# Row-tiled attention scores, with the second GEMM split into row halves among them and the attention-times-V work gathered into one stretch per pair of heads

One core of a Trainium2 chip. The metric is the device time of one execution in microseconds (us), median of several runs. The notes on the chip that are quoted as "the Trainium skill" are a set of pages; each is named by its title where it is used.

## The reference

Forgetting attention for 8 batches x 8 heads, 576 tokens, head size 64, feeding a two-layer network with exact GELU on the 4608 resulting rows:

```python
scores = q @ k.T / sqrt(64)
decay  = cum[..., :, None] - cum[..., None, :]      # cum = cumsum(log f)
attn   = softmax(where(causal, -1e9, scores + decay))
x      = (attn @ v)  -> rows of 512 (8 heads x 64)
out    = gelu(x @ w_in) @ w_out                     # 512 -> 2048 -> 512
```

Inputs and output are fp32; the kernel multiplies in bf16 and accumulates in fp32.

## The kernel before

Batches go through TensorE one after another. A batch has two stages: its attention, among whose matmuls the second GEMM of the batch before is strewn as filler so that TensorE hardly waits for the exponentials, and then its first GEMM. Heads are handled in pairs, because two heads of 64 fill the 128 partitions. The scores of a pair use one stationary tile of k for both heads; the q of either head is padded with zeros in the other head's half:

```python
# scores(b, i, t): tile t of pair i
for n, q0, w in STILES[t]:
    for h, qt in enumerate((qA[i], qB[i])):          # zero-padded halves
        nc.tensor.matmul(st[:, h, c:c+w], kT[i][:, K0[n]:K0[n]+P],
                         qt[:, q0:q0+w], start=True, ...)
...
nc.scalar.activation(et[:, :, 0:c], st[:, :, 0:c], Act.Exp, scale=scale)
```

The filler counts say how many second-GEMM matmuls follow each score tile; the attention-times-V work ("AV", 15 matmuls a head) is spread over three places of the next pair:

```python
FILL = [[4, 6, 2, 2], [2, 2, 2, 2], [2, 2, 2, 2], [2, 2, 1, 1], [8, 0, 20]]
# attention(b, fill, counts)
for i in range(HP):
    for t in range(4):
        scores(b, i, t)
        if i and t == 1:   attend(b, i - 1, 0, (0, 1, 2))
        elif i and t == 2: attend(b, i - 1, 0, (3, 4));          normalize(b, i - 1, 0)
        elif i and t == 3: attend(b, i - 1, 1, (0, 1, 2, 3, 4)); normalize(b, i - 1, 1)
        ...
        take(fill, counts[i][t])
```

The pools take eight banks of PSUM, the buffer that matmuls write to: two score tiles of two banks each, two banks for AV, two for the GEMMs. A pool hands a buffer on when its last reader is done.

The softmax here doesn't subtract the row's maximum and nothing guards it: scores larger than these inputs give would overflow.

## Time and profile before

| | before |
|---|---|
| median | 356.84 us (356.57 to 357.11) |
| TensorE busy | 97% of the span |
| a steady batch (first score to first score, batch 3) | 37.42 us |
| of which attention with filler / first GEMM | 23.53 / 13.89 us |
| ScalarE (exponentials, GELU) busy in a steady batch | 25.2 us |

The steady batch is the unit to read: batches 3 to 6 repeat it to 0.01 us, and batch 7 repeats its attention. Its rows, and the lines about mode switches and exponentials, stand in the prediction.

### The profile page before, as it was taken

The page shows a single profiled execution, that of the slowest core. Times are in us where ns is not written, and L with a number is a line of the kernel's source. Part 1 is how long each engine was busy: PE and PEld are TensorE (multiplying, and loading weights), DVE is VectorE, ACT ScalarE, POOL GpSimd, SP SyncE. Part 2 cuts the span into 40 slices and gives each one's busy share as a digit, 9 for nine tenths or more (in the row PEclk, how much of TensorE's full clock was granted, in tenths as well). Part 3 has the DMA queues.
Part 4 walks back from the last instruction along what each step waited for, and adds up shares of the span by engine and source line. Part 5 has one row for each costly group of instructions (what it writes and reads, how often), then busy time and mean ns, then how long its engine had stood idle before and what let it go on. Part 6 is the DMA issues. An engine that isn't in the chain of part 4 may idle for free.

```text
span 356.2 us, 7069 instructions
## 1 busy us (share of the span) xinstructions
PE 346.8 (97%) x2756; PEld 190.7 (54%) x2756; DVE 182.1 (51%) x482; ACT 217.4 (61%) x298; POOL 124.5 (35%) x243
## 2 busy tenths in 40 slices
PE   8998989999999999999999999999999999999995
PEld 3784556544664466445654565446544664444443
DVE  6771984595467625781559145924584361011011
ACT  5697586368854797279826882688457854603600
POOL 7390275406546044804470256215520530000000
PEclk9999999999999999999999999999999999999999
DMA  7999999885997894489639973979310132011013
GB/s 116 169 188 191 190 155 202 183 192 90 205 158 161 146 185 122 95 142 189 144 98 134 188 139 82 174 141 173 76 66 2 45 61 81 2 59 59 2 30 88
DMA packets 103936, 43.85 MB, mean 123 GB/s; under 512 B 82720, under 2 KB 99360, under 8 KB 103904
## 3 DMA queue, kind: packets, MB, share of 16 engines
q1 hardware_dynamic: 86608, 29.26, 40.4%
q0 software_dynamic: 16896, 13.63, 25.6%
q10 hardware_dynamic: 400, 0.52, 0.4%
q8 instruction: 21, 0.34, 0.4%
q14 instruction: 11, 0.09, 0.1%
HBM read 36.85 MB, written 9.44 MB: 130 GB/s over the span
## 4 chain that ended last, share of the span: by engine, by line
PE 94%; ACT 2%; DMA 1%; issue 1%; DVE 1%; POOL 0%; ACTq 0%; DVEq 0%; POOLq 0%
PE ps L404 35%; PE ps L442 35%; PE s L308 13%; PE o L344 8%; ACT e L323 2%; PE ps_f L198 1%; DMA k<-in_k_dram 1%; PE s L317 1%; PE ps_w L187 1%; PE ps_x L380 0%; PE s_t L233 0%; PE ps_t L233 0%; DVE x L360 0%; ACT xt L368 0%; ACT g L416 0%
## 5 line engine op out<-in xcount | busy, mean ns | idle before, releaser
L416 ACT ACTIVATE g<-ps 128x512 bf16<-128x512 f32 x144 | 86.0, 597 | 97.9 <-PE ps L404 97.8
L442 PE MATMUL ps<-w_out_sb,g 128*128 128x512 bf16 (+2 forms) x592 | 143.8, 373 | 0.0
L323 ACT ACTIVATE e<-s 128x896 bf16<-128x896 f32 (+1 forms) x128 | 105.1, 863 | 19.8 <-PE s L308 11.3
L404 PE MATMUL ps<-xT,w_in_sb 128*128 128x512 bf16 x512 | 112.9, 379 | 0.7 <-ACT xT L383 0.6
L325 POOL TENSOR_SCALAR_AFFINE_SELECT e<-e 128x256 bf16<-128x256 bf16 x135 | 53.7, 408 | 118.6 <-ACT e L323 117.7
L404 PEld LDWEIGHTS <-w_in_sb 128*128 128x128 bf16 x576 | 56.0, 97 | 69.2 <-issue 3.9
L451 DVE COPY ot<-ps 128x512 f32<-128x512 f32 (+2 forms) x37 | 25.1, 677 | 105.3 <-PE ps L442 105.0
L442 PEld LDWEIGHTS <-g 128*128 128x128 bf16 x592 | 52.2, 98 | 41.8
L292 POOL TENSOR_TENSOR vw<-v_sb,wT 128x640 bf16<-128x640 f32 x32 | 41.0, 1282 | 45.7 <-PE ps_t L233 15.9
L308 PEld LDWEIGHTS <-kT 128*128 128x128 bf16 x384 | 36.7, 98 | 33.3 <-issue 6.2
L308 PE MATMUL s<-qA,kT 128*128 128x256 bf16 (+2 forms) x192 | 51.9, 282 | 2.1 <-ACT e L323 2.0
L308 PE MATMUL s<-qB,kT 128*128 128x256 bf16 (+2 forms) x192 | 48.6, 282 | 0.0
L344 PE MATMUL o<-vw,e 128*128 128x65 bf16 x960 | 43.5, 194 | 0.5 <-ACT e L323 0.4
L344 PEld LDWEIGHTS <-e 128*128 128x128 bf16 x960 | 39.5, 98 | 7.5 <-ACT e L323 0.5
L359 DVE RECIPROCAL r<-o 128x5 f32<-128x5 f32 x64 | 12.5, 195 | 41.5 <-PE o L344 41.0
L276 DVE COPY kT<-tk 64x288 bf16<-64x288 bf16 x96 | 32.3, 336 | 1.4
L360 DVE TENSOR_TENSOR x<-o,r 128x256 bf16<-128x256 f32 x64 | 27.2, 425 | 2.4 <-DVE r L359 0.2
L276 DVE COPY qB<-tq 64x288 bf16<-64x288 bf16 x48 | 18.8, 391 | 0.6
L370 DVE TENSOR_SCALAR xt<-o,r 64x64 bf16<-64x64 f32 x60 | 17.5, 291 | 1.4
L276 DVE COPY qA<-tq 64x288 bf16<-64x288 bf16 x48 | 17.1, 355 | 1.1
L404 PE MATMUL ps<-tails,w_in_sb 128*128 128x512 bf16 x64 | 14.4, 377 | 0.0
L416 ACT ACT_TABLE_LOAD x8 | 10.3, 1283 | 0.1
(63 smaller groups left out, 124.4 us busy)
## 6 DMA issues: line engine op xcount, KB each, us to landing
out_dram<-ot SPq DMA_DIRECT2D x32, 256.0 KB, 2.2
v_sb<-in_v_dram SPq DMA_DIRECT2D x20, 256.0 KB, 4.7
v_sb<-in_v_dram SPq DMA_DIRECT2D x29, 128.0 KB, 5.4
q<-in_q_dram POOLq DMA_DIRECT2D x6, 576.0 KB, 6.6
k<-in_k_dram POOLq DMA_DIRECT2D x6, 576.0 KB, 9.0
w_in_sb<-in_moe_w_in_dram POOLq DMA_DIRECT2D x4, 512.0 KB, 7.6
w_out_sb<-in_moe_w_out_dram POOLq DMA_DIRECT2D x4, 512.0 KB, 9.6
q<-in_q_dram POOLq DMA_DIRECT2D x4, 144.0 KB, 4.1
```

The source lines that it names most:

```text
L276: nc.vector.tensor_copy(rows[:, odd], src[odd * D : (odd + 1) * D, 2 * i + h].rearrange("d j p -> d p j"),)
L292: nc.gpsimd.tensor_tensor(vw_of[b][:, hs, :, 0:D], v_sb[:, hs, :, :], w.unsqueeze(3).to_broadcast([P, 2, NBLK, D]), Alu.mult,)
L308: nc.tensor.matmul(st[:, h, c : c + w], kT[i][:, K0[n] : K0[n] + P], qt[:, q0 : q0 + w], start=True, stop=not on_pe or c not in SDIAG[t],)
L323: nc.scalar.activation(et[:, :, 0:c], st[:, :, 0:c], Act.Exp, scale=scale)
L325: nc.gpsimd.affine_select(out=et[:, :, c0 : c0 + P], in_=et[:, :, c0 : c0 + P], compare_op=Alu.is_ge, fill=0.0, base=0, pattern=[[0, 2], [ ...
L344: nc.tensor.matmul(o[:, m, :], e_of[b, i, t][:, h, c : c + P], vw_of[b][:, 2 * i + h, n, :], start=(n == 0), stop=(n == m),)
L360: nc.vector.tensor_tensor(x_of[b, i][:, :, h, :], o[:, 0:4, 0:D], r[:, 0:4].unsqueeze(2).to_broadcast([P, NBLK - 1, D]), Alu.mult,)
L370: nc.vector.tensor_scalar(*tail, r[D:P, 4:5], None, Alu.mult)
L404: nc.tensor.matmul(ps, w_in_sb[:, kt, ffb * P : (ffb + 1) * P], src[:, kt, :], start=(kt == 0), stop=(kt == n_dm - 1),)
L416: nc.scalar.activation(g_of[c][ffb], ps, Act.Gelu)
L442: nc.tensor.matmul(pss[ts][:, c0:c1], g_of[c][kt][:, ts * P : (ts + 1) * P], w_out_sb[:, kt, c0:c1], start=(kt == 0), stop=(kt == n_ff - 1),)
L451: nc.vector.tensor_copy(ot[:, c0:c1], pss[ts][:, c0:c1])
```

## The change

The intent: two heads' scores each need only 64 rows of the array. Put on the two row halves, they can run side by side and take half the time, and the padding goes. Since a change between 64-row and 128-row work costs something, the second GEMM's steps among the scores are split as well, into two 64-row halves that accumulate in two banks and are added by VectorE; and the AV work, which needs all 128 rows, is gathered into one stretch per pair, with unsplit steps inside it.

```diff
-            for h, qt in enumerate((qA[i], qB[i])):
+            for h in range(2):
+                d = slice(h * D, (h + 1) * D)
                 nc.tensor.matmul(
                     st[:, h, c : c + w],
-                    kT[i][:, K0[n] : K0[n] + P],
-                    qt[:, q0 : q0 + w],
+                    kT[i][d, K0[n] : K0[n] + P],
+                    qT[i][d, q0 : q0 + w],
 ...
+    STEPS = [16 * "r", "rrrrrrrnnrrrrrnn", "rrrrrrrrrrnnrrrr", 8 * "r" + 8 * "n"]
+    def gemm2_rows(c):
+        for ts, steps in enumerate(STEPS):
+            # two banks: block 0 in the AV pool, 1 and 2 in the GEMM pool, 3 in a score tile
 ...
+            for kt, step in enumerate(steps):
+                last = kt == steps.rindex("r")
+                for r in range(2 if step == "r" else 1):
+                    rows = slice(r * D, (r + 1) * D) if step == "r" else slice(0, P)
+                    nc.tensor.matmul(banks[r], g_of[c][kt][rows, ...], w_out_sb[rows, kt, :], ...)
+                if last:
+                    nc.vector.tensor_copy(ot, banks[1])
+                if kt == n_ff - 1:
+                    nc.vector.tensor_tensor(ot, ot, banks[0], Alu.add)
 ...
+    FILL = [[6, 6, 4, 4], [0, 3, 1, 1], [0, 3, 3, 3], [1, 3, 2, 2], [8]]
+    FILL_AV = [2, 2, 2, 2]
+        def av(i):
+            for h in range(2):
+                attend(b, i, h, (0, 1, 2, 3, 4))
+                normalize(b, i, h)
+                if h == 0:
+                    take(fill, FILL_AV[i])
 ...
+                scores(b, i, t)
+                take(fill, FILL[i][t])
+                if i and t == 1:
+                    av(i - 1)
 ...
+        take(fill, FILL[HP][0])
+        av(HP - 1)
+        take(fill, 6)
+        to_xT(b, HP - 1, nc.vector.tensor_copy, o_psum, "o")
```

Batches 0 and 1 keep their old order (batch 1 as a function of its own, with the unsplit GEMM) and only get the row-tiled scores; the zero fills and half of the q evacuations (copies out of PSUM) go. One more thing moves: from batch 3 on, the kernel before sent the last pair's x through a DMA transpose; now TensorE transposes it (`to_xT`, four matmuls) and VectorE copies the result.

More of the change, by code (lines that the diff above doesn't have):

```diff
@@ L142 @@
     make_identity(nc, ident_fp)
-    qA = [consts.tile([P, S], BF16, name=f"qA{i}") for i in range(HP)]
-    qB = [consts.tile([P, S], BF16, name=f"qB{i}") for i in range(HP)]
+    qT = [consts.tile([P, S], BF16, name=f"qT{i}") for i in range(HP)]
     kT = [consts.tile([P, S], BF16, name=f"kT{i}") for i in range(HP)]
-    def zero_halves(pairs):
-        for i in pairs:
-            nc.vector.memset(qA[i][D:P, :], 0.0)
-            nc.vector.memset(qB[i][0:D, :], 0.0)
     w_in_sb = consts.tile([P, n_dm, d_ff], BF16)
@@ L174 @@
     nc.vector.memset(ones, 1.0)
-    zero_halves(range(2))
     nc.vector.memset(wT[0:D, 4, :], 0.0)
@@ L202, in transposes_first @@
                 )
-        def evac(eng, dst, r0, r1):
-            op = eng.copy if eng is nc.scalar else eng.tensor_copy
-            op(
-                dst[r0:r1, :].rearrange("d (p j) -> d p j", j=JT),
-                ps[r0:r1].rearrange("d j p -> d p j"),
-            )
-        if which:
-            evac(nc.vector, kT[i], 0, P)
-        else:
-            evac(nc.vector if i else nc.scalar, qA[i], 0, D)
-            evac(nc.vector, qB[i], D, P)
+        op = nc.scalar.copy if i == 0 and not which else nc.vector.tensor_copy
+        op(
+            (qT, kT)[which][i].rearrange("d (p j) -> d p j", j=JT),
+            ps.rearrange("d j p -> d p j"),
+        )
     def transposes_pe(b, i, pool):
@@ L239, in transposes_pe @@
             for h in range(2):
-                dst = (qA[i], qB[i])[h] if which == 0 else kT[i]
+                dst = (qT, kT)[which][i]
                 rows = dst[h * D : (h + 1) * D, :].rearrange(
@@ L270, in untangle @@
             for h in range(2):
-                dst = (qA[i], qB[i])[h] if which == 0 else kT[i]
+                dst = (qT, kT)[which][i]
                 rows = dst[h * D : (h + 1) * D, :].rearrange(
@@ L461, in gemm2 @@
             yield
+    STEPS = [16 * "r", "rrrrrrrnnrrrrrnn", "rrrrrrrrrrnnrrrr", 8 * "r" + 8 * "n"]
+    def gemm2_rows(c):
+        for ts, steps in enumerate(STEPS):
+            if ts < n_sub - 1:
+                pool, tag = (m_psum, "m") if ts else (o_psum, "o")
+                banks = [
+                    pool.tile([P, d_model], FP32, tag=tag, name="ps2")
+                    for _ in range(2)
+                ]
+            else:
+                both = s_psum.tile([P, 2, d_model], FP32, tag="s", name="ps2")
+                banks = [both[:, 0], both[:, 1]]
+            ot = o_pool.tile([P, d_model], FP32, tag="ot", name="ot")
+            for kt, step in enumerate(steps):
+                last = kt == steps.rindex("r")
+                for r in range(2 if step == "r" else 1):
+                    rows = slice(r * D, (r + 1) * D) if step == "r" else slice(0, P)
+                    nc.tensor.matmul(
+                        banks[r],
+                        g_of[c][kt][rows, ts * P : (ts + 1) * P],
+                        w_out_sb[rows, kt, :],
+                        start=(kt == 0),
+                        stop=last if r else kt == n_ff - 1,
+                    )
+                if last:
+                    nc.vector.tensor_copy(ot, banks[1])
+                if kt == n_ff - 1:
+                    nc.vector.tensor_tensor(ot, ot, banks[0], Alu.add)
+                    nc.sync.dma_start(
+                        out[c * S + ts * P : c * S + (ts + 1) * P, :], ot
+                    )
+                yield
     def take(gen, n):
@@ L481, in first_attention @@
         transposes(0, o_psum, "o")
-        zero_halves(range(2, HP))
         warm_up(4)
@@ L534, in first_attention, with attention, second_attention @@
         to_xT(0, 3, nc.vector.tensor_copy)
-    FILL = [[4, 6, 2, 2], [2, 2, 2, 2], [2, 2, 2, 2], [2, 2, 1, 1], [8, 0, 20]]
+    FILL = [[6, 6, 4, 4], [0, 3, 1, 1], [0, 3, 3, 3], [1, 3, 2, 2], [8]]
+    FILL_AV = [2, 2, 2, 2]
     FILL_1 = [[0, 4, 4, 0], [0, 2, 3, 3], [4, 4, 4, 4], [3, 3, 3, 3], [8, 0, 99]]
-    def attention(b, fill, counts):
+    def attention(b):
+        fill = gemm2_rows(b - 1)
+        def av(i):
[4 more added lines that the diff above has]
+                    take(fill, FILL_AV[i])
+        for i in range(HP):
+            for t in range(4):
+                scores(b, i, t)
+                take(fill, FILL[i][t])
+                if i and t == 1:
+                    av(i - 1)
+                    if i < HP - 1 or b > 2:
+                        x_dma(b, i - 1)
+                if t == 1 and i == 0:
+                    load_v(b + 1)
+                if b > 2 and t == 0 and i < 2:
+                    transpose_dma(b + 1, 4 * i, 4 * i + 4)
+                if b == 2 and t == 1 and i == 1:
+                    transpose_dma(3, 0, 4)
+                    transpose_dma(3, 4, 8)
+        take(fill, FILL[HP][0])
+        if b == 2:
+            to_xT(b, HP - 2, nc.vector.tensor_copy, o_psum, "o")
+        av(HP - 1)
+        take(fill, 6)
+        to_xT(b, HP - 1, nc.vector.tensor_copy, o_psum, "o")
+        x_tail_dma(b)
+        take(fill, 999)
+    def second_attention():
+        b, fill, counts = 1, gemm2(0, True), FILL_1
         for i in range(HP):
@@ L552, in attention @@
                     normalize(b, i - 1, 1)
-                    if i < HP - 1 or b > 2:
+                    if i < HP - 1:
                         x_dma(b, i - 1)
-                if t == 1 and i == 0 and b > 1:
-                    load_v(b + 1)
-                if b > 2 and t == 0 and i < 2:
-                    transpose_dma(b + 1, 4 * i, 4 * i + 4)
-                if b == 2 and t == 3 and i == 1:
-                    transpose_dma(3, 0, 4)
-                    transpose_dma(3, 4, 8)
-                if b == 1 and (i, t) == (0, 2):
+                if (i, t) == (0, 2):
                     transposes_pe(1, 3, o_psum)
-                if b == 1 and i == 1 and t in (0, 2):
+                if i == 1 and t in (0, 2):
                     weigh_v(1, 2 + t // 2)
-                if b == 1 and t == 3:
+                if t == 3:
                     if i == 1:
@@ L573, in attention @@
         take(fill, counts[HP][0])
-        if b <= 2:
-            to_xT(b, i - 1, nc.vector.tensor_copy, o_psum, "o")
+        to_xT(b, i - 1, nc.vector.tensor_copy, o_psum, "o")
         attend(b, i, 0, (0, 1, 2, 3, 4))
@@ L580, in attention @@
         normalize(b, i, 1)
-        if b <= 2:
-            take(fill, 7)
-            to_xT(b, i, nc.vector.tensor_copy, o_psum, "o")
-        else:
-            x_dma(b, i)
+        take(fill, 7)
+        to_xT(b, i, nc.vector.tensor_copy, o_psum, "o")
         x_tail_dma(b)
-        if b == 1:
-            transpose_dma(2, 4, 8)
-            load_v(2, 4, 8)
+        transpose_dma(2, 4, 8)
+        load_v(2, 4, 8)
         take(fill, 999)
@@ L594 @@
             first_attention()
+        elif b == 1:
+            second_attention()
         else:
-            attention(b, gemm2(b - 1, b == 1), FILL_1 if b == 1 else FILL)
+            attention(b)
         if b == 0:
```

## The prediction

> **What bounds the kernel now.** I read the page first (busy shares, the chain that ended last), then busy time by stage, then one steady stage instruction by instruction.
>
> ```profile
> PE 346.8 (97%) x2756; PEld 190.7 (54%) x2756; DVE 182.1 (51%) x482; ACT 217.4 (61%) x298; POOL 124.5 (35%) x243
> PE 94%; ACT 2%; DMA 1%; issue 1%; DVE 1%; POOL 0%; ACTq 0%; DVEq 0%; POOLq 0%
> ```
>
> The chain is TensorE (PE) almost throughout: first GEMM (line 404) 35%, second GEMM (line 442) 35%, scores (line 308) 13%, attention times V ("AV", line 344) 8%. By stage:
>
> ```profile
> core 0: us, PE busy (x) PEld busy (x) DVE busy (x) ACT busy (x) POOL busy (x), PEclk, DMA share, GB/s
> 0.00:11.10 11.10, 9.41 (x70) 4.95 (x71) 7.32 (x17) 5.57 (x6) 7.08 (x19) 1.00 0.88 134
> 11.10:28.70 17.60, 15.44 (x269) 12.57 (x269) 13.81 (x33) 14.71 (x21) 12.14 (x18) 1.00 1.09 175
> 44.50:71.30 26.80, 25.27 (x263) 15.72 (x261) 16.84 (x45) 16.64 (x19) 16.04 (x30) 1.00 1.03 180
> 146.90:160.80 13.90, 13.90 (x67) 6.29 (x65) 11.86 (x33) 8.96 (x15) 3.09 (x5) 1.00 0.81 144
> 160.80:184.30 23.50, 23.50 (x234) 14.24 (x232) 9.37 (x27) 16.23 (x19) 12.11 (x26) 1.00 0.78 137
> ```
>
> The first two rows are batch 0's attention, the third batch 1's with the second GEMM of batch 0 as filler. The last two are a steady batch, repeated six times (batches 2 to 7): 13.9 us of first GEMM, then 23.5 us of attention filled with the second GEMM. There PE never pauses; everybody else does. Work on PE is what sets a steady stage, though ScalarE's (ACT's) 16.23 us of exponentials and tables is not far below. A busy PE record overlaps its neighbours, so I cost PE by start-to-start distances: 13.89 us for 64 matmuls of 512 columns is 0.217 each (512 columns at 2.4 per ns is 0.213); 15 AV matmuls take 0.48.
>
> Two further details matter. How fast ACT can run, and how long a change of array shape takes:
>
> ```profile
> 162.76 1.73 ACT L323 ACTIVATE e<-s 128x896 bf16<-128x896 f32 x2
> ```
> ```profile
> 11.40 0.28 PE L317 MATMUL s<-after,ident_bf 128*128 128x128 bf16 x2
> 11.61 0.52 PE L489 MATMUL psw<-ident_fp,f_sb 64*128 64x64 f32 x5
> ...
> 12.95 0.27 PE L317 MATMUL s<-after,ident_bf 128*128 128x128 bf16 x2
> 13.15 0.47 PE L198 MATMUL ps_f<-ident_bf,k 96*64 96x96 bf16 x10
> ...
> 14.13 0.28 PE L317 MATMUL s<-after,ident_bf 128*128 128x128 bf16 x2
> 14.24 0.25 PE L308 MATMUL s<-qA,kT 128*128 128x192 bf16 x1
> ```
>
> One wide exponential lasts 0.92, so two in 1.73 start 0.81 apart. Two 128-column mask matmuls should occupy 0.11, as they do ahead of line 308 (14.13 to 14.24). Ahead of the 64-row fp32 matmuls and of the 64-column transposes the distance is 0.21 and 0.20: about **0.10 us more when the shape of the array changes**.
>
> **What the Trainium skill says.** "TensorEngine Tiling (Array Packing)", Key Properties: changing the tiling mode, not merely the tile, drains TensorE. No duration is given; the 0.10 above agrees. The same page, Gotcha 1: different row tiles must write different PSUM banks, which is why the changed GEMM takes two banks per block. "TensorE: Matmul & The Clock Gate", Measured speedup vs the span model: a packed group takes one matmul's time plus about 4 ns per further tile. No concurrent pair exists in the trace before, so I take the 4 ns from there. "PSUM — Partial Sum Buffer", PSUM bank collisions: readers and writers of a bank must be kept apart by semaphores; so a block's banks come free only after VectorE's (DVE's) last read, and that becomes important below.
>
> **The change part by part, one steady stage.**
>
> *Scores.* Each pair of heads has per head 256+192+320+128+448+320 = 1664 columns, now two zero-padded 128-row matmuls in a row. Two heads: 2 x (1664/2.4 + 6 x 2.5 ns) = 1.42 us; as concurrent 64-row tiles 0.73 us. Four pairs: **-2.7 us**.
>
> *Second GEMM.* 50 of its 64 steps become two 64-row halves in two banks: the same 0.217 us each plus 4 ns, +0.2 us. They do no work faster; they keep the array in row mode among the scores.
>
> *Mode switches.* Into row mode at the stage's start, out and back round three AV stretches, out for the fourth: 8 x 0.10 = **+0.8 us**.
>
> *DVE.* Per token block one more 512-column pass (copy one bank, add the other): 4 x 0.69 = +2.8 us on an engine 40% busy. Harmless in sum, not where the next step waits for it.
>
> So by sum a stage falls by 1.7 us, six stages by 10 us. But the order changes too, so I laid the stage out, time 0 at its first score. Rules from the stage before: score finished issuing to exponential 0.29 (169.81 to 170.10); exponential end to the score reusing its buffer 0.05; AV end to DVE 0.19; normalization 0.95; first exponential at 2.11 (last GELU, then table load of 1.28).
>
> - Pair 0, 20 steps, ends at 5.2. The exponentials keep up.
> - Pair 1: scores 0 and 1, three steps, AV from 6.4 to 7.8. Before, the two AV halves lay between different scores. Now score 2 waits behind 3 steps + 30 AV matmuls + 2 steps + two switches, about 2.2 us, while two exponentials cover 1.6. **ACT starves about 1 us**, and the next pair's first two scores then wait 0.7 and 0.4 for their PSUM buffers, with only one filler step between.
> - Pair 2: AV ends at 12.3. The next step is the first of block 2, whose banks are block 1's. DVE runs normalization of head 0 (11.5 to 12.5) before block 1's add (to 13.2). **PE waits 0.7**.
> - Pair 3 to 18.8; the 8 steps of block 3 need a score buffer: 0.2 of waiting, then to 20.8.
> - Last AV with 2 steps, 6 more to 23.6, transposes to 23.8. DVE does the last add (to 24.4) before it copies the transposed x (to 24.9); the first GEMM's fourth matmul needs it and could have run at 24.4: **0.5 lost**.
>
> Stalls: 0.7+0.4+0.7+0.2+0.5 = 2.5. Stage: 23.53 - 2.7 + 0.2 + 0.8 + 2.5 = 24.3 against 23.53, so **+0.75, six times: +4.5 us**.
>
> *Batch 1* keeps the unsplit second GEMM among row-tiled scores: roughly 16 score groups with two switches each, 32 x 0.10 = 3.2 against 2.7 saved: +0.5.
> *Batch 0.* The zero fills (8 x 0.30 on DVE) and three evacuations of 0.76 go. The first score, however, waits for PE's own warm-up (four matmuls of 0.43 from 6.99 to 8.70, the score at 8.67), so the start hardly moves. Row-tiled scores at the slow early pace save 0.4, later ones hide behind exponentials: about -0.5.
> *After batch 7* nothing changes. Sum: 356.8 + 4.5 + 0.5 - 0.5 = 361.3.
>
> **The rivals.**
> (1) *PE's sum wins.* If the tuned placement avoids the stalls, six stages gain 1.7 each: 346 to 348. For it: PE is 23.50 of 23.50 busy and loses 2.7 us of work a stage; whoever chose the steps (five in pair 1, twenty in pair 0) probably tuned them by measurement. Against it: each stall follows from in-order engines and two-buffer pools.
> (2) *ACT becomes the bound.* 2.11 + 13 exponentials' worth (16 exponentials, 4 x (3 x 0.81 + 0.6) = 12.1) + AV, 8 steps and transposes after it (2.9) is 17.2, well under 23. So not its busy time, only its starvation counts.
> (3) *Row tiles don't run side by side fully*, or a switch costs more where a weight load must follow it. Each 0.10 more per switch is 0.8 a stage plus 3 in batch 1, 8 in all: 369. Nothing in the profile before shows a concurrent pair, so this stays open.
>
> **Range and chances.** The layout says 361; rival 1 pulls down by up to 14 and deserves about a fifth, rival 3 pulls up. I put it at 360, with 347 to 369 holding it 8 times in 10. Two per cent is 7.1 us: under 349.7 is faster, over 364.0 slower. Faster 0.19, within 0.55, slower 0.26.
>
> **What would show it.** Right: a steady attention stretch (first score to first GEMM) of 24 to 25 us, with pauses of PE before the first scores of pairs 2, before block 2's first step and in the first GEMM's first group, waiting for ACT, DVE and DVE; score pairs 0 to 10 ns apart; about 0.10 at each change of rows. Wrong: a stretch under 22.5 us with no such pauses (rival 1), row steps well over 0.22 us or switches of 0.2 (rival 3), or batches 0 and 1 moving by more than 2 us.

## The result, and the profile after

The changed kernel took 361.62 us (360.75 to 362.45), against 356.82 for the kernel before in the same rounds: ratio 1.0134, 95% interval 1.0106 to 1.0162. Ratios here and below are the mean time of one kernel's fast runs over that of the other's of the same rounds, so not quite the ratio of the medians. All profiled runs are fast ones; of the others one was slow (x_tail's run of 363.73 us, at a granted clock of 0.981), and it is in that median but not in the ratio.

The page's chain (by engine, then by line), after:

```profile
PE 83%; DVE 7%; ACT 5%; issue 2%; DMA 1%; POOL 0%; ACTq 0%; POOLq 0%
PE ps L392 34%; PE ps L474 21%; PE ps L430 11%; PE s L296 7%; PE o L332 6%; ACT e L311 5%; DVE ot L484 2%; DVE ot L482 2%; PE s L305 1%; PE ps_f L192 1%; DMA k<-in_k_dram 1%; DVE x L348 1%; DVE xT L371 1%; PE ps_w L181 1%; DVE xt L358 0%
```

The scores (now line 296) fell from 13% to 7%, as intended. But 94% TensorE became 83%: VectorE (7%) and ScalarE (5%) now stand in the path that sets the end. The same steady batch, cut at its first score and its first GEMM matmul (columns as in the prediction's table):

```profile
162.41:186.27 23.86, 22.49 (x287) 12.82 (x287) 12.40 (x34) 16.06 (x19) 9.14 (x21) 1.00 0.84 150
186.27:200.58 14.31, 14.07 (x67) 6.17 (x65) 13.81 (x33) 8.96 (x15) 6.19 (x10) 1.00 0.65 107
```

Attention lasts 23.86 instead of 23.53, and TensorE is no longer busy all through it; the first GEMM lasts 14.31 instead of 13.89. Together 38.17 against 37.42: 0.75 more, in each of the batches 3 to 6. Where the time lies idle shows in the order of time. Pairs 1 and 2 of that batch (start, length, instruction, and in brackets the idle time before it and what ended it):

```profile
168.58 0.65 PE L332 MATMUL o<-vw,e 128*128 128x65 bf16 x15
169.07 0.59 PE L474 MATMUL ps<-w_out_sb,g 128*128 128x512 bf16 x2
169.50 0.64 PE L332 MATMUL o<-vw,e 128*128 128x65 bf16 x15
...
170.07 0.36 PE L296 MATMUL s<-qT,kT 64*128 64x448 bf16 x2
...
170.53 3.18 ACT L311 ACTIVATE e<-s 128x896 bf16<-128x896 f32 x4 [0.88 <-PE s L296]
...
171.50 0.37 PE L296 MATMUL s<-qT,kT 64*128 64x256 bf16 x4 [0.50 <-ACT e L311]
172.10 0.37 PE L296 MATMUL s<-qT,kT 64*128 64x320 bf16 x4 [0.23 <-ACT e L311]
...
174.73 0.38 PE L474 MATMUL ps<-w_out_sb,g 64*128 64x512 bf16 x1
174.74 0.69 DVE L484 TENSOR_TENSOR ot<-ot,ps 128x512 f32<-128x512 f32 x1
...
175.48 0.80 PE L474 MATMUL ps<-w_out_sb,g 64*128 64x512 bf16 x5 [0.37 <-DVE ot L484]
```

The third score tile of pair 1 starts at 170.07, behind the whole AV stretch. ScalarE has run out and waits 0.88; it pays back by making TensorE wait for score buffers at 171.50 and 172.10. At 174.73 block 2 of the second GEMM begins; its second half needs the bank that VectorE is still adding from, and goes on at 175.48. (The brackets count idle time from the modelled end of a matmul; start to start, the three pauses are 0.66, 0.41 and 0.54 us. The third costs 0.2 more a little later: the two halves run on one step apart, and are nearly together again only when a score tile of pair 3 has waited for an exponential, at 177.27.) The end of the attention and the start of the first GEMM:

```profile
183.00 0.65 PE L332 MATMUL o<-vw,e 128*128 128x65 bf16 x15
183.11 0.69 DVE L482 COPY ot<-ps 128x512 f32<-128x512 f32 x1 [0.56 <-PE ps L474]
...
183.85 0.59 PE L474 MATMUL ps<-w_out_sb,g 128*128 128x512 bf16 x2 [0.20 <-DVE ot L482]
...
186.25 0.69 DVE L484 TENSOR_TENSOR ot<-ot,ps 128x512 f32<-128x512 f32 x1 [0.32 <-PE ps L474]
186.27 0.81 PE L392 MATMUL ps<-xT,w_in_sb 128*128 128x512 bf16 x3
186.86 0.42 DVE L371 COPY xT<-ps_x 128x512 bf16<-128x512 bf16 x1
...
187.32 0.38 PE L392 MATMUL ps<-xT,w_in_sb 128*128 128x512 bf16 x1 [0.24 <-DVE xT L371]
```

Three matmuls of the first GEMM run, then the fourth waits until 187.32 for the copy of the transposed x, which stood behind the add of 0.69 on VectorE: 0.40 lost. Another 0.37 is lost ahead of 183.85 (AV started at 183.00 and its 15 matmuls take 0.48): the unsplit steps of block 3 wait for VectorE to have copied the other bank of the same two-bank score tile. One more pause is hidden where two groups of steps are merged in a long view. Two shorter windows show it:

```profile
180.50 0.59 PE L474 MATMUL ps<-w_out_sb,g 64*128 64x512 bf16 x4
...
181.17 1.26 PE L474 MATMUL ps<-w_out_sb,g 64*128 64x512 bf16 x10
```

Two steps start at 180.50 and 180.72, and the next, the first of block 3, only at 181.17 instead of 180.93: it needs the score tile whose exponential ends at 181.1. That is 0.23 lost.

### The profile page after: what moved, and what is told of

Read it like the earlier page. It is cut to its first block, busy times and chain, and to the rows that moved or that the text cites. A ratio compares the mean times of both kernels' runs of the same rounds, so it can differ in the third digit from the quotient of the medians.

```text
span 360.7 us, 7705 instructions
## 1 busy us (share of the span) xinstructions
PE 342.0 (95%) x3076; PEld 175.4 (49%) x3076; DVE 204.2 (57%) x499; ACT 216.3 (60%) x298; POOL 124.9 (35%) x243
## 4 chain that ended last, share of the span: by engine, by line
PE 83%; DVE 7%; ACT 5%; issue 2%; DMA 1%; POOL 0%; ACTq 0%; POOLq 0%
PE ps L392 34%; PE ps L474 21%; PE ps L430 11%; PE s L296 7%; PE o L332 6%; ACT e L311 5%; DVE ot L484 2%; DVE ot L482 2%; PE s L305 1%; PE ps_f L192 1%; DMA k<-in_k_dram 1%; DVE x L348 1%; DVE xT L371 1%; PE ps_w L181 1%; DVE xt L358 0%
## 5 line engine op out<-in xcount | busy, mean ns | idle before, releaser
L474 PE MATMUL ps<-w_out_sb,g 64*128 64x512 bf16 (+1 forms) x684 | 104.6, 376 | 3.7 <-DVE ot L484 2.2
L474 PEld LDWEIGHTS <-g 64*128 64x128 bf16 (+1 forms) x684 | 38.3, 94 | 32.0 <-issue 8.7
L296 PE MATMUL s<-qT,kT 64*128 64x320 bf16 (+4 forms) x384 | 47.3, 282 | 6.6 <-ACT e L311 6.4
L263 DVE COPY qT<-tq 64x288 bf16<-64x288 bf16 x96 | 46.5, 484 | 1.5
L430 PE MATMUL ps<-w_out_sb,g 128*128 128x512 bf16 (+2 forms) x208 | 44.3, 363 | 0.0
L482 DVE COPY ot<-ps 128x512 f32<-128x512 f32 x24 | 16.6, 692 | 39.2 <-PE ps L474 39.2
L439 DVE COPY ot<-ps 128x512 f32<-128x512 f32 (+2 forms) x13 | 8.5, 650 | 50.0 <-PE ps L430 49.9
L296 PEld LDWEIGHTS <-kT 64*128 64x128 bf16 x384 | 19.6, 94 | 29.7 <-issue 19.3
L430 PEld LDWEIGHTS <-g 128*128 128x128 bf16 x208 | 18.8, 98 | 18.9 <-issue 0.4
L484 DVE TENSOR_TENSOR ot<-ot,ps 128x512 f32<-128x512 f32 x24 | 16.5, 688 | 2.4 <-PE ps L474 1.8
```

What stands on the lines that cost most here:

```text
L263: nc.vector.tensor_copy(rows[:, odd], src[odd * D : (odd + 1) * D, 2 * i + h].rearrange("d j p -> d p j"),)
L296: nc.tensor.matmul(st[:, h, c : c + w], kT[i][d, K0[n] : K0[n] + P], qT[i][d, q0 : q0 + w], start=True, stop=not on_pe or c not in SDIAG[t],)
L430: nc.tensor.matmul(pss[ts][:, c0:c1], g_of[c][kt][:, ts * P : (ts + 1) * P], w_out_sb[:, kt, c0:c1], start=(kt == 0), stop=(kt == n_ff - 1),)
L474: nc.tensor.matmul(banks[r], g_of[c][kt][rows, ts * P : (ts + 1) * P], w_out_sb[rows, kt, :], start=(kt == 0), stop=last if r else kt == n ...
L482: nc.vector.tensor_copy(ot, banks[1])
```

## The experiments

My theory: the row tiling does what it should; the 2.7 us that it saves in a batch are spent on eight switches of about 0.10 and on the new pauses (2.8 us by the list above), which come from the order of the work and not from the tiling. The rivals: switches or row tiles cost more than the trace suggests; or ScalarE has become a true bound, so that no order helps. Four groups of runs: the pauses one by one; the switch by itself; the order without the tiling; and a mended order. "Period" is the time from the first score of batch 3 to that of batch 4 in the profiled run (before 37.42, changed 38.17).

**The transposed x ahead of the add.**

```diff
-        take(fill, 6)
+        take(fill, 5)
         to_xT(b, HP - 1, nc.vector.tensor_copy, o_psum, "o")
         x_tail_dma(b)
         take(fill, 999)
```

> The changed kernel, with the four transposes of the last pair put ahead of the last filler step instead of behind it, so that VectorE copies the transposed x before it does block 3's last add. My theory (the first GEMM's fourth matmul waits for a copy that stands behind an add on VectorE): the pause of about 0.5 us at the start of each steady first GEMM goes, 6 times 0.5 is 3 us, 358.6 us. Rival (the pause is hidden by something else, for instance the DMA transposes of the earlier pairs landing late): within 1 us of 361.6.

Measured: 358.75 us, ratio to before 1.0041 (1.0013 to 1.0069), period 37.77: 0.40 less, just the pause. VectorE's copy now comes first and the first GEMM runs through:

```profile
184.38 0.42 DVE L371 COPY xT<-ps_x 128x512 bf16<-128x512 bf16 x1 [0.32 <-PE ps_x L368]
184.39 2.97 PE L392 MATMUL ps<-xT,w_in_sb 128*128 128x512 bf16 x13
184.83 0.69 DVE L484 TENSOR_TENSOR ot<-ot,ps 128x512 f32<-128x512 f32 x1
```

**The add ahead of the normalization.**

```diff
                 attend(b, i, h, (0, 1, 2, 3, 4))
-                normalize(b, i, h)
                 if h == 0:
                     take(fill, FILL_AV[i])
+                normalize(b, i, h)
```

> The changed kernel, with the normalization of head 0 issued behind the two filler steps inside the AV stretch, so that block 1's add stands before it on VectorE. My theory: the pause of 0.4 to 0.7 us of TensorE before block 2's second step in pair 2 shrinks to under 0.2 us, in six stages some 3 us less, 358.5 us. Rival (TensorE is then held back by starved exponentials of the same pair anyway, so the pause only moves): within 1 us of 361.6.

Measured: 359.78 us, ratio 1.0059 (1.0036 to 1.0082), period 37.60: 0.57 less. The add now starts 0.36 us ahead of the third score tile, where before it started 0.21 behind it, and the pause has shrunk to a fraction (three steps in six halves show 0.98, where the same six show 0.82 undisturbed):

```profile
171.99 0.69 DVE L484 TENSOR_TENSOR ot<-ot,ps 128x512 f32<-128x512 f32 x1 [0.33 <-PE ps L474]
172.35 0.36 PE L296 MATMUL s<-qT,kT 64*128 64x448 bf16 x2
172.55 0.98 PE L474 MATMUL ps<-w_out_sb,g 64*128 64x512 bf16 x6
```

**The AV stretch behind the third score tile.**

```diff
-                if i and t == 1:
+                if i and t == 2:
                     av(i - 1)
-    FILL = [[6, 6, 4, 4], [0, 3, 1, 1], [0, 3, 3, 3], [1, 3, 2, 2], [8]]
+    FILL = [[6, 6, 4, 4], [0, 3, 0, 2], [0, 3, 0, 6], [1, 3, 0, 4], [8]]
```

> The changed kernel, with the AV stretch of a pair behind the third score tile instead of the second; number of steps, of mode switches and the steps within the stretch unchanged. My theory (ScalarE starves because the third score tile waits behind the stretch): the idle 0.9 us of ScalarE in pair 1 and the waits of TensorE for exponentials before pair 2 (0.5 and 0.2) shrink, but the wait for block 1's add stays and ScalarE then starves before the fourth tile for some 0.7: about 0.3 us a stage less, 360 us. Rival (starved exponentials are the main loss): over 1 us a stage less, under 356 us.

Measured: 360.45 us, ratio 1.0090 (1.0068 to 1.0113), period 37.96: 0.21 less. The stretch, with two filler steps in it, is still too long for the one exponential that it now leaves in reserve; the starvation moved to the fourth tile.

**The three together.**

> The three moves of the runs before together, row tiling, step kinds and mode switches untouched. My theory: the losses are separate, 0.5 (tail) + 0.5 (add) + 0.3 (stretch) a stage, about 8 us in all, 353.6 us, so a little under the kernel before. Rival (switches and row tiles cost more than I think and the waits hide them): no less than the better of the single moves, 358 us or more.

Measured: 355.15 us, ratio 0.9954 (0.9915 to 0.9994), period 37.00: 1.17 less, the sum of the three (0.40 + 0.57 + 0.21 = 1.18). The pauses are separate. (The median is 1.5 us above what I expected, and the interval is wide: two of its six runs took 359.5 and 356.1. The profiled one was that of 359.5; its granted clock dipped within the first 36 us, ahead of the batches in question.) Nothing in the tiling was touched, and the loss is gone: the first rival falls as the main cause.

**Fourteen more switches.** Block 0 alternates between split and unsplit steps; the multiply-adds stay the same.

```diff
-    STEPS = [16 * "r", ...
+    STEPS = ["rnrnrnrnrnrnrnrr", ...
```

> The changed kernel with 7 of the 16 steps of block 0 unsplit, alternating with split ones: 14 more mode switches a stage, same multiply-adds, same order. My theory: 14 x 0.10 = 1.4 us a stage, six stages 8.4 us, 370 us. Rival (switches are hidden by overlap with weight loads): within 2 us of 361.6. A switch of 0.2 us would give 378.

Measured: 371.32 us, ratio 1.0378 (1.0328 to 1.0428), period 39.65: 1.48 more for 14 switches, **0.106 us each**. The 0.10 read from the trace before holds, and it isn't hidden.

**Row-tiled scores alone,** in the order of the kernel before, with its unsplit GEMM (the diff of `scores` above, with qT in place of qA and qB, and the zero fills and copies that go with it).

> The kernel before, in its own order and with its unsplit second GEMM, with row-tiled scores alone. My theory (0.10 us at each change of rows): each of 16 score groups of a steady stage is entered and left, 32 x 0.10 = 3.2 us against 2.7 saved, +0.5 a stage, +3 in six; batches 0 and 1 as in the changed kernel, +0.9; 360.7 us. Rival (a switch costs next to nothing where weights are loaded ahead): 16 us less, 341 us. Rival (row tiles do not run side by side): the scores save nothing, 377 us.

Measured: 359.61 us, ratio 1.0042 (1.0020 to 1.0064), period 37.76, 0.34 more than before. The time of the first switches shows in the trace:

```profile
160.60 0.38 PE L392 MATMUL ps<-xT,w_in_sb 128*128 128x512 bf16 x1
160.91 0.36 PE L296 MATMUL s<-qT,kT 64*128 64x256 bf16 x4
161.20 1.04 PE L430 MATMUL ps<-w_out_sb,g 128*128 128x512 bf16 x4
```

From the last 512-column matmul to the first score it is 0.31 where 0.21 would be the matmul itself; and four row-tiled scores of 256 and 192 columns, 0.19 us of columns when side by side, are followed after 0.29. Both rivals fall: the scores do run in pairs, and the 32 switches eat up what that saves (32 x 0.10 = 3.2 against 2.7).

**The order alone,** with full-width zero-padded scores throughout and the unsplit GEMM (`fill = gemm2(b - 1)`).

> The changed kernel's order of the steady batches (one AV stretch a pair, twenty steps in pair 0) with full-width zero-padded scores and the unsplit second GEMM in its usual banks: no row tiling and no mode switches. My theory: the order alone costs, by starved exponentials in each pair some 0.8 us and by the late copy of the transposed x 0.5 us, 1.0 to 1.5 us a stage, 363 to 366 us. Rival (the order is harmless, row tiling brings the waits by making TensorE faster than ScalarE): within 1 us of the kernel before.

Measured: 363.74 us, ratio 1.0153 (1.0126 to 1.0181), period 38.45, 1.03 more than before without any row tiling in it. ScalarE waits for scores in this batch:

```profile
172.32 3.35 ACT L323 ACTIVATE e<-s 128x896 bf16<-128x896 f32 x4 [1.04 <-PE s L308]
...
173.28 0.27 PE L308 MATMUL s<-qA,kT 128*128 128x256 bf16 x1 [0.36 <-ACT e L323]
```

So the order makes waits without any tiling; the tiling merely got less out of it than it could. (0.22 of the 1.03 is no wait but the last pair's transposes, which this run has on TensorE too.)

**A mended version.** As the three moves together, and besides: no filler inside the AV stretch, so that it lasts 1.2 us with its switches and ScalarE's reserve nearly covers it; the steps spread so that block 1 ends just before the AV stretch of pair 2 and VectorE's two passes lie under that stretch; all unsplit steps behind the last AV. Switches remain eight a batch.

```diff
-    STEPS = [16 * "r", "rrrrrrrnnrrrrrnn", "rrrrrrrrrrnnrrrr", 8 * "r" + 8 * "n"]
+    STEPS = [16 * "r", 16 * "r", 16 * "r", 8 * "r" + 8 * "n"]
-    FILL = [[6, 6, 4, 4], [0, 3, 1, 1], [0, 3, 3, 3], [1, 3, 2, 2], [8]]
-    FILL_AV = [2, 2, 2, 2]
+    FILL = [[6, 6, 4, 4], [0, 5, 0, 2], [2, 3, 0, 2], [3, 3, 0, 8], [8]]
+    FILL_AV = [0, 0, 0, 0]
-        take(fill, 6)
+        take(fill, 7)          # then to_xT, then the last step
```

> Row tiling and number of switches as in the changed kernel; AV behind the third score tile and with no filler step inside it, the steps moved into the pairs so that block 1 ends just before the AV stretch of pair 2 and its two VectorE passes lie under that stretch, the unsplit steps of block 3 all behind the last AV, normalization behind the adds, transposes before the last step. By laying it out with the durations of the trace: score to first GEMM 21.6 us instead of 24.3, 35.5 us a batch against 37.4 before; six batches 11 us less, 346 us, faster than before by 3%. Rival (a wait that I do not see takes its place, or ScalarE binds): 352 us or more.

Measured: 348.60 us, ratio 0.9734 (0.9710 to 0.9759): faster than before. The period is 35.52, as laid out. But the time is 2.6 us above what I expected, and most of it lies in batch 2, which took 38.24 us instead of 35.52. There VectorE waits for a buffer of x:

```profile
DVE x L348 <- DMA xT<-x: 2.5, 1, 2.5
...
PE ps_x L368 <- DVE x L348: 1.9, 1, 1.9
```

(who waited for whom, us in total, times, longest.) x has three buffers; pair 3 needs that of pair 0, which is free when a DMA has transposed it. By moving the AV stretch to the third tile I had put that transpose behind the four transposes for batch 3 in the queue.

**The transposes for batch 3 queued behind that of pair 0's x.**

```diff
-                if b == 2 and t == 1 and i == 1:
+                if b == 2 and t == 2 and i == 1:
                     transpose_dma(3, 0, 4)
                     transpose_dma(3, 4, 8)
```

> The mended version with one line moved: in batch 2 the two transposes for batch 3 are queued behind the transpose of pair 0's x instead of before it. In the mended version batch 2 alone took 38.2 us instead of 35.5, with VectorE waiting 2.5 us for that transpose to free an x buffer. My theory: batch 2 falls to about 35.6 us, 346 us. Rival (batch 2 is long for another reason): within 1 us of 348.6.

Measured: 348.53 us, ratio 0.9751 (0.9710 to 0.9792). A miss: batch 2 took 37.80 us instead of 38.24, and the whole hardly moved. The wait had changed its place: pair 1's x was now the one behind the four transposes.

```profile
PE ps L392 <- DMA xT<-x: 1.4, 1, 1.4
```

**One pair later still** (`i == 2`).

> As the run before, with the two transposes for batch 3 queued one pair later still, behind the transpose of pair 1's x as well. In the run before batch 2 took 37.8 us because the first GEMM then waited 1.4 us for pair 1's x, queued behind these transposes. My theory: that wait goes, batch 2 falls to 36.0 to 36.5 us, about 347 us. Rival (the transposes for batch 3 now land too late for batch 2's first GEMM stage, where VectorE untangles them, or another transfer is held up): no gain, 348 us or more.

Measured: **345.85 us** (345.76 to 347.26), ratio **0.9675** (0.9653 to 0.9697), batch 2 at 36.22. This is the fastest version, 3.2% under the kernel before and correct. Its steady batch:

```profile
157.82:179.44 21.62, 21.62 (x294) 12.89 (x294) 12.48 (x34) 15.99 (x19) 9.59 (x23) 1.00 0.96 167
179.44:193.34 13.90, 13.90 (x65) 6.15 (x64) 13.38 (x33) 8.96 (x15) 5.76 (x8) 1.00 0.66 108
```

TensorE is busy all through again, 21.62 us instead of 23.53: that is 1.9 less, about the 2.7 of the scores minus eight switches (the transposes add 0.22, and 0.26 of waits that pair 0 had before are gone). ScalarE is busy 16.0 of these 21.6, so the second rival (ScalarE as a bound) falls too.

**What the mended order is worth without the tiling, and what the split is worth.** Two more runs take the mended order (before the moves of the transposes) with full-width scores and unsplit GEMM, and with row-tiled scores but unsplit GEMM.

> The order of the mended version with full-width zero-padded scores and the unsplit second GEMM: no row tiling, no switches. My theory (the order decides about waits only; with no waits TensorE's sum remains, and that is what it was before): 23.5 to 23.8 us of attention a stage, 357 to 359 us, like the kernel before. Rival (the new order is by itself better than the old and row tiling adds little): 353 us or less.

Measured: 358.86 us, ratio 1.0043 (1.0010 to 1.0077), period 37.52: about as good as the old order, no better.

> The mended version with row-tiled scores but the unsplit second GEMM among them. My theory: some 30 switches a stage instead of 8, at 0.10 each 2.2 us more, 13 us in six stages, 361 to 362 us. Rival (splitting the second GEMM is not needed, the order made the gain): within 2 us of 348.6.

Measured: 361.24 us, ratio 1.0109 (1.0083 to 1.0135), period 37.87: 2.35 more than with the split, for some 22 more switches, 0.107 each.

All of it in one table (period of a steady batch, us; in brackets the median time; the kernel before took 356.8 to 357.9):

| order | full-width, unsplit | row-tiled scores, unsplit GEMM | row-tiled, split GEMM |
|---|---|---|---|
| of before | 37.42 (356.8) | 37.76 (359.6) | not run |
| of the change | 38.45 (363.7) | not run | 38.17 (361.6) |
| mended | 37.52 (358.9) | 37.87 (361.2) | 35.52 (348.6; 345.9 with batch 2 mended) |

In the mended order the gain needs both row tiles (fewer columns) and the split (few switches), and with both it needs an order without waits. What the split would give in the order of before was not run. In the order of the change the tiling is worth 0.28 us a batch, in the mended one 2.00.

## Why the prediction was right

The time (361.6 against 360 on record and 361.3 by the layout), the direction and the cause, pauses that the order brings, came out as worked out. That the sum came so close is in part luck: the steady batches bring 3.5 us and not the 4.5 of the layout, and batches 0 and 1 together about 1 us and not none (batch 2 starts at 86.06 instead of 85.09). Of what it named as signs, the attention stretch of 24 to 25 us was not quite met (23.86); the layout's own 24.3 contains the 0.5 that is lost in the first GEMM. Point by point:

- *Scores.* Right. Side by side, tiles of 448 columns now issue in 0.19 us for both heads.
- *Second GEMM's half-steps.* The 4 ns did not add up from pair to pair. The second half of a pair does start 0.003 to 0.004 us after the first, but in the chain of the changed kernel 12 halves take 1.29 us, 0.215 a pair, the same as one full matmul (four of these took 0.86 in the chain before). The +0.2 was 0. From that chain, after (start, length, work):

```profile
162.78 1.29 PE ps L474 x12
```

- *Mode switches.* 0.10 predicted from two places in the trace before, 0.106 and 0.107 measured by two runs that changed their number in an otherwise equal order (the second of them also drops the split and its adds).
- *Starvation in pair 1.* Predicted 0.7 and 0.4 of waiting for TensorE, measured 0.66 and 0.41. *Block 2's bank.* Predicted 0.7, measured 0.54 and 0.2 more later. *Late x copy.* Predicted 0.5, measured 0.40 by the trace and by the run that removed it.
- *Block 3's score buffer.* Predicted 0.2, measured 0.23. What the layout missed is the 0.37 before block 3's unsplit steps: they write one bank of a two-bank tile while VectorE copies the other, and the dependence is kept for the tile as a whole. (In block 1, whose banks are two tiles, the unsplit steps start at 173.53, while VectorE copies from 173.15 to 173.84.)
- *The sum of a stage.* The prediction's sum leaves out the 0.22 of the transposes, and "there PE never pauses" was not quite so: in pair 0 of the stage before, two score tiles start 0.15 and 0.11 late, each 0.05 after the end of the exponential that frees their buffer. From the starts, after minus before: scores -2.76, switches +0.84, transposes +0.22, seven pauses +2.8, those two waits -0.26; that is about 0.85, against 0.75 measured. The prediction's 0.75 came out because what it miscounted nearly cancels.
- *A steady batch.* Predicted +0.75, measured +0.75 in batches 3 to 6, and +0.5 from batch 7's first score to the end. Batch 2 took 38.18, within 0.04 of its 38.14 before, so it contributed none: I counted six such batches, and instead of 4.5 us they bring 3.5.
- *Batch 1.* Predicted +0.5, measured about +0.5 (its first GEMM starts 0.88 later than before, of which 0.35 was there at the end of batch 0).
- *Batch 0.* Predicted -0.5; no gain is seen. In this pair of profiles its first GEMM starts at 29.10 instead of 28.75, but profiles of one and the same code for batch 0 differ by more: 28.75, 28.09 and 27.59 with full-width scores, 27.61 to 29.10 in eight with row tiles at full clock. From the first score to the first GEMM it is 19.79 to 20.36 and 20.12 to 21.24, so rather longer than shorter. The step that failed is "row-tiled scores at the slow early pace save 0.4, later ones hide behind exponentials": I had left out that the mask matmuls of this batch use all 128 rows, so each of the five diagonal tiles of a pair adds two switches, 1.0 us against 0.7 saved. The trace shows these switches (13.99 to 14.21 for two mask matmuls that take 0.11); what they cost the batch was not run by itself.

```profile
13.99 0.29 PE L305 MATMUL s<-after,ident_bf 128*128 128x128 bf16 x2
14.21 0.26 PE L296 MATMUL s<-qT,kT 64*128 64x192 bf16 x2
```

- *The rivals.* Rival 1, that TensorE's smaller sum wins, was given a fifth and is what the mended version shows to be possible; the placement in this change did not do it. Rival 2 and rival 3 are refuted by the runs. For rival 3 the trace before held more than I saw: in batch 0 two tiles already work side by side, by columns. The 24 transposes between 13.15 and 13.76 (96*64 in the view) go to two column halves and start 0.026 us apart on average, where 96 columns one after another would take 0.04 at the pace of the mask matmuls (128 in 0.056).

## What to carry to other kernels

When the engine that sets the time gets faster, lay out one steady period by hand from start-to-start distances: the saved work is real only if the engines that feed it and free its buffers keep up in that order, and a long uninterrupted stretch starves whoever has only two buffers of reserve. Count how often the array changes its row mode before tiling by rows; here 32 changes of 0.10 us undid a halving of the scores, and splitting the neighbouring matmuls to the same rows cost nothing on TensorE and brought the count down to 8. After each move in an in-order queue, ask what now stands behind what: adds before copies, and transposes before the one that frees a buffer, were worth 0.4 us in each batch and 2.0 us once (batch 2).

## What the Trainium skill lacked or had wrong

- "TensorEngine Tiling (Array Packing)", Key Properties, says that a change of mode drains TensorE, but not how long: here 0.10 to 0.11 us per change (1.48 us for 14, 2.35 us for about 22), in either direction.
- "TensorE: Matmul & The Clock Gate", Measured speedup vs the span model, gives about 4 ns for each further tile of one packed group, and the trace agrees (0.003 to 0.004 us between the two starts). It does not say whether this adds up from group to group: for pairs of 64-row tiles of 512 columns it does not, 0.215 us a pair as for one full matmul.
- That page (Part 3, The mechanism) has matmuls start in program order, and no page says what happens when one tile of a pair is held up. In the changed kernel the second half of a step waited for its bank from 174.73 to 175.48, and afterwards the halves ran on one step apart, the second half of one step beside the first half of the next, at the same pace; the two halves of the next score tile start 0.20 us apart instead of together. By the recorded starts each row half then keeps its own order, and program order is not kept between the halves: below, the half-step at 176.06 stands behind both score matmuls in the program and starts before the second of them.

```profile
175.92 0.30 PE L296 MATMUL s<-qT,kT 64*128 64x320 bf16 x1
176.06 0.38 PE L474 MATMUL ps<-w_out_sb,g 64*128 64x512 bf16 x1
176.12 0.29 PE L296 MATMUL s<-qT,kT 64*128 64x320 bf16 x1
```
